# Placing the small Fourier sets of a fused filter and mixer next to each other on TensorE

## Chip, cores and metric

One NeuronCore of one Trainium2 chip runs the kernel. The metric is the device time in microseconds (us), from launch to end. The profile is one execution of the program, recorded by the hardware profiler. Everything is fp32.

## What is computed

The input x has 8 batches of 3008 tokens with 256 channels. First comes a global filter along the tokens (a real Fourier transform, a product with a learned complex filter, and the inverse transform), then one mixer layer:

```
X = np.fft.rfft(x, axis=1)
y = np.fft.irfft(X * (filt_r + 1j * filt_i), n=3008, axis=1)
h = relu(yT @ w_tok1) @ w_tok2          # across the tokens, 3008 -> 256 -> 3008
u = y + hT
out = u + relu(u @ w_ch1) @ w_ch2       # across the channels, 256 -> 1536 -> 256
```

## The kernel before

**The filter.** 3008 is 47 x 64. A set of length-64 sums runs first (`a_pair`), its result goes through DRAM, and then 16 pairs of frequency rows each get a forward length-47 set (`b_pair`), the product with the filter (the two VectorE instructions of line 674), a joining of the parts (`join`, lines 679 and 680) and an inverse length-47 set (`bi_pair`). The inverse set's two result banks are copied out by ScalarE (`by_block`, line 660), and SyncE's DMA queue writes them to DRAM (line 689). Each set is four small matmuls on the four quarters of the TensorE array (`four`, line 523); each takes both banks called `acc` and `b` in the order of `turn`. The length-64 sets have the same shape. The rest of the inverse transform is folded into the mixer's matmuls.

**The mixer.** The channel products use a seven-product scheme for 2x2 blocks (Strassen-Winograd), so a matrix product is seven matmuls with sums on VectorE before and after. The work is cut into 288 **items**: 8 batches, 6 token blocks m (the last of 448 columns, the others of 512), and 6 pairs of hidden tiles jp. Item i, in program order, does these things on TensorE: `up_first` (four matmuls, line 936) into two PSUM banks of the pool `pg`, which has exactly two buffers; `down` part 0 of the item before (three, line 970); `up_last` (three, line 952) into the same two `pg` banks; `down` part 1 of the item before (four, line 970). TensorE takes two passes for each fp32 matmul, and the profile has one record for a pass; an item thus has 28.

Beside it VectorE, whose sums all have line 914, does for each item: `up_middle` (two sums that read the `pg` banks, the first behind a ScalarE copy of line 939), `h_sums` (three sums that make the tile `t` for `down` part 1), and in `up_last` two sums that read the two `pg` banks into `hh`, each followed by a ReLU on ScalarE (line 957). The `pg` banks are free for the next item once these two are done.

**Once per block.** The next block's `u` tile is made in four **quarters** (`u_quarter`, lines 835 and 857, in banks `acc` and `b`), with sums on VectorE behind them, and then the steps `v_steps` (two, three sums). When a block ends, `finish` queues six **combining steps** `a`, `b_`, `c`, `d`, `turn(0)` and `store`; the last two are transposes (line 1002), and `store` issues the 16 output DMAs (line 1017). Queued steps are taken from the list `todo_v` by `one_step()`: one ahead of `h_sums`, one behind `up_last`, and two when a block's last `down` has been issued.

**The order.** Nothing reorders the program: it is written out by hand under `manual_schedule`. `mix` is a generator that yields after each third of an item (places 0, 1 and 2: after `down` part 0, after `up_last`, after `down` part 1), and the loop at the file's end uses those yields to advance another generator, `dft`, which makes the filter of the next group of batches. The groups are (0), (1, 2), (3, 4), (5, 6), (7). The filter of batches 1 and 2 runs in batch 0's items by a table of its own (its sets are of another form). The filters of (3, 4), (5, 6) and (7) run in batches 1 to 6. There `dft` says what is coming (`"a"` a length-64 set, `"w"` loads, `"b"` a forward set, `"m"` a joining, `"i"` an inverse set), and a table of (jp, place) says where it is due. Per block there are two pairs: forward sets at (5, 1) and (2, 1), joinings at (0, 1) and (3, 0), inverse sets at (1, 0) and (3, 2). In a batch's last block, "tail" below, one forward set comes at (1, 1). The quarters are at (3, 0), (4, 0) and (4, 2). In the tail of all batches but the last the token product of the next batch (line 802, 168 passes) runs at (2, 2), with its own sums on VectorE, and the quarters of the next batch's first block at (4, 0) and (5, 0).

The tiles that matter: `p1p` and `p2p`, the products' two halves, have one buffer each; the joining writes its result into the `p1p` tile, and the inverse set reads it from there. Tables (`wbp`) and filter rows have three buffers, the length-47 inputs (`t2p`) and the outputs (`t3p`) two.

Of the kernel before, what the change touches and what calls it, by code (L numbers as in the profile page):

```python
# [127 lines left out]
def kernel(  # L128
# [428 lines left out]
    def dft(bs):  # L557
# [102 lines left out]
            nc.scalar.copy(out=out.rearrange("p b (e g i) -> p b g e i", e=DH, i=CW),  # L660
                           in_=ps.rearrange("p b (g e i) -> p b g e i", e=DH, i=CW))

        def two_banks():
            return [bank(tag).rearrange("p (b d) -> p b d", b=2)[:, 0:nb, :] for tag in turn]

        def b_pair(c):
            pss, wb, t2 = two_banks(), wbs[c], t2s[c]
            four(lambda h, i: pss[h][half_of(i)], lambda h, i: wb[half_of(h, KH), i], lambda h, i: t2[half_of(h, KH), i])  # L670
            where = (p1p, p2p)
            for h in range(2):
                prods[c, h] = where[h].tile([P, 2, nb, D], FP32, tag="p%d" % (h + 1), name="p%d" % (h + 1))
                nc.vector.tensor_tensor(out=prods[c, h], in0=pss[h].unsqueeze(1).to_broadcast([P, 2, nb, D]),
                                        in1=filts[c % FB][:, :, 0, :].unsqueeze(2).to_broadcast([P, 2, nb, D]), op=ALU.mult)
# [3 lines left out]
            nc.vector.tensor_tensor(out=p1[:, 0], in0=p1[:, 0], in1=p2[:, 1], op=ALU.subtract)  # L679
            nc.vector.tensor_tensor(out=p1[:, 1], in0=p1[:, 1], in1=p2[:, 0], op=ALU.add)  # L680

        def bi_pair(c):
            pss, wb, p = two_banks(), wbs[c], prods.pop((c, 0))
            four(lambda i, h: pss[i][half_of(h)], lambda i, h: wb[half_of(i), 2 + h], lambda i, h: p[half_of(i), h])
            t3 = t3p.tile([P, KC, nb, D], FP32, tag="t3", name="t3")
            for i in range(KC):
                by_block(t3[:, i], pss[i])
            for h in range(2):
                nc.sync.dma_start(g_d[place_of[bs[0]][0]][ts(c, KC), ts(h, KH)].rearrange("k r b d -> r k b d"),
                                    t3[half_of(h, KH)])  # L690
# [8 lines left out]
        yield "w"  # L699
        yield "b"  # L700
        if not first:
            for c in range(K2 // KC):
                b_pair(c)
                if c + 2 < K2 // KC:
                    t2_load(c + 2)
                    w_load(c + 2)
                yield "m"
                join(c)
                yield "i"
                bi_pair(c)  # L710
                if c + 1 < K2 // KC:
                    yield "b"
            return
        if first:
# [244 lines left out]
    def down(m, jp, part, hh, t, po):  # L959
        hw = width(m) // 2  # L960
        if not po:
            for i in range(4):
                po.append(bank("po%d" % i).rearrange("p (s n) -> p s n", s=2))
        b11, b21, b22 = (hh[:, i, 0:hw] for i in (0, 3, 2))
        t1, t3, t2, t4_ = (t[:, i, 0:hw] for i in range(4))

        todo = (((0, 0, 1, 0, 1, b21), (0, 1, 0, 1, 2, b22), (2, 0, 1, 0, 0, b11)),
                ((1, 1, 1, 0, 6, t1), (3, 0, 1, 1, 4, t3), (2, 1, 0, 1, 5, t2), (1, 0, 0, 1, 3, t4_)))
        for i, j, first, last, n, mov in todo[part]:
            nc.tensor.matmul(po[i][:, j, 0:hw], chan[1][:, jp, n, :], mov, start=(jp == 0 and first == 1),  # L970
                             stop=(jp == JP - 1 and last == 1))
# [70 lines left out]
    def one_step():  # L1042
        if todo_v:
            todo_v.pop(0)()

    def mix(next_ready):

        wait = []
        pos, hhs, tts = {}, {}, {}

        def loads(b):
            if b + 1 < B and next_ready(b):
                for c in wait:
                    t4_load(b + 1, c)
                wait.clear()


        own = ({(4, 2): (0, 1)}, {(3, 0): (0,), (4, 0): (1,), (4, 2): (2, 3)})
        new = {(JP - 2, 0): (0, 1), (JP - 1, 0): (2, 3)}

        def u_parts(b, m, jp, place):
            parts = own[b > 0] if m + 1 < MT else new if b + 1 < B else {}
            now = parts.get((jp, place), ())
            b, m = (b, m + 1) if m + 1 < MT else (b + 1, 0)
            for part in now:
                u_part(b, m, part)
            if now and now[-1] == max(p for ps in parts.values() for p in ps):
                if m:
                    wait.append(m)
                todo_v.extend(v_steps(b, m))  # L1070
                if b and (b, m) < (B - 1, MT - 2):
                    w2m_load((m + 2) % MT)

        to_dram = [f for m in range(MT) for f in w2_sums(m)]
        w1_todo, w1_out = w1_sums()
        items = [(b, m, jp) for b in range(B) for m in range(MT) for jp in range(JP)]
        n = MT * JP
        for i in range(len(items) + 1):
            now, old = i < len(items), i >= 1
            if JP - 2 <= i < JP + 2:  # L1080
                for _ in range(6 if i > JP - 2 else 1):
                    if w1_todo:
                        w1_todo.pop(0)()
            elif i >= 2 * JP and i % 2 and w1_out:
                w1_out.pop(0)()
            if i and ended[0] < len(tiles):
                convert_middle()
                convert_end(False)
                convert_middle()
            if now:  # L1090
                b, m, jp = items[i]
                if i % n == 0:
                    wait.append(0)
                w = width(m)
                hhs[i] = hp.tile([P, 4, 256], FP32, tag="hh", name="hh")
                g = [bank("pg").rearrange("p (s n) -> p s n", s=2) for _ in range(2)]
                s = up_first(jp, uts[b, m], vts[b, m], w, g)
                up_middle(hhs[i], w, g, s)
            while todo_h1:
                todo_h1.pop()()  # L1100
            one_step()
            if old:
                bo, mo, jo = items[i - 1]
                tts[i - 1] = tp.tile([P, 4, 256], FP32, tag="t", name="t")
                for f in h_sums(hhs[i - 1], tts[i - 1], width(mo)):
                    f()
                down(mo, jo, 0, hhs[i - 1], tts[i - 1], pos.setdefault((bo, mo), []))
            if now:
                u_parts(b, m, jp, 0)
            copies()  # L1110
            yield b, i % n, 0
            if ended[0] < len(tiles):
                if i == 0:
                    convert_middle()
                convert_end(False)
            if now:
                up_last(jp, uts[b, m], vts[b, m], w, g, s, hhs[i])
                if b + 1 < B and i % n == n - 4:
                    t4_sums(b + 1, 0)
            one_step()  # L1120
            if now and i % n == n - 1:
                one_step()
            if now and b + 1 < B:
                if n - 4 - W1S <= i % n < n - 4:
                    w1_load(i % n - (n - 4 - W1S))
                if i % n == n - 4:
                    t4_sums(b + 1, 1)
            copies()
            loads(b)
            yield b, i % n, 1  # L1130
            if old:
                down(mo, jo, 1, hhs.pop(i - 1), tts.pop(i - 1), pos[bo, mo])
                if jo == JP - 1:
                    todo_v.extend(finish(bo, mo, uts[bo, mo], pos[bo, mo]))
                    one_step()
                    one_step()
            if now:
                if b + 1 < B and i % n == n - 4:
                    h1s[b + 1] = token_product(b + 1)
                u_parts(b, m, jp, 2)  # L1140
                if jp == JP - 1:
                    while todo_v and m + 1 == MT:
                        one_step()
                if i >= 8 and to_dram:
                    to_dram.pop(0)()
                if i in (28, 29):
                    w2m_load(i - 28)
            loads(b)
            yield b, i % n, 2
        while todo_v:  # L1150
            one_step()

    with tc.manual_schedule():
# [70 lines left out]
        for b, i, place in mix(next_ready):  # L1224
# [8 lines left out]
                continue  # L1233
            jp = i % JP
            if coming in "aw":
                due = place == 1 or group == 0
            elif group:
                due = (jp, place) in {"b": ((5, 1), (1 if i >= n - JP else 2, 1)), "m": ((0, 1), (3, 0)), "i": ((1, 0), (3, 2))}[coming]
            else:
                due = (jp - (coming == "i")) % JP in ((5, 1, 2, 3) if i < 4 * JP else (5, 0, 1, 2, 3)) and place == {"b": 1, "m": 2, "i": 0}[coming]  # L1240
            if coming == "a" and group == 0 and i < JP - 1:
                due = (2, 0, 1)[place]
            for _ in range(due):
                if not done:
                    coming = next(todo, "end")
# [31 lines left out]
```

## Time and profile before

| | |
|---|---|
| Time, median of 3 runs | 2445.72 us (2444.69 to 2446.33) |
| Profiled execution: time, span | 2445.61 us, 2443.8 us |
| Granted TensorE clock, mean | 0.995 |
| TensorE matmul busy | 2399.8 us in 12340 passes |
| VectorE busy | 1937.0 us |
| ScalarE busy | 687.0 us |
| GpSimd busy | 621.0 us |
| Items of batches 1 to 7 | 476.8 to 2425.0 us of the span |

The span runs from the first instruction to the last; the launch adds 1.8 us outside it. The items of batch 0, with the filter of batches 1 and 2 and the conversion of weights between them, fill the span up to 476.8 us. An item's length is read in the timeline as the distance between two starts of `ps_pg<-u` on line 936, the first passes of `up_first`.

In a timeline line the first number is the start in us from the span's start, the second the length in us, then the engine (PE is TensorE, DVE VectorE, ACT ScalarE), the line, the operation, its output and inputs, sizes, and how many instructions were merged. A bracket gives idle time of the engine ahead of the line, and what ended it. In a list of waits each line is: engine, the line waiting, the work waited for, us in total, times, longest.

### The profile page before, as it was taken

The page shows a single profiled execution, that of the slowest core. Times are in us where ns is not written, and L with a number is a line of the kernel's source. Part 1 is how long each engine was busy: PE and PEld are TensorE (multiplying, and loading weights), DVE is VectorE, ACT ScalarE, POOL GpSimd, SP SyncE. Part 2 cuts the span into 40 slices and gives each one's busy share as a digit, 9 for nine tenths or more (in the row PEclk, how much of TensorE's full clock was granted, in tenths as well). Part 3 has the DMA queues.
Part 4 walks back from the last instruction along what each step waited for, and adds up shares of the span by engine and source line. Part 5 has one row for each costly group of instructions (what it writes and reads, how often), then busy time and mean ns, then how long its engine had stood idle before and what let it go on. Part 6 is the DMA issues. An engine that isn't in the chain of part 4 may idle for free.

```text
span 2443.8 us, 35574 instructions
## 1 busy us (share of the span) xinstructions
PE 2399.8 (98%) x12340; PEld 1971.9 (81%) x12340; DVE 1937.0 (79%) x3684; ACT 687.0 (28%) x1355; POOL 621.0 (25%) x1115
## 2 busy tenths in 40 slices
PE   7999999999999999999999999999999999999998
PEld 4666676978788877987888878897889888898887
DVE  7798788787887788778878887877787787777776
ACT  5733223132222222123222222213221222212222
POOL 7476332122112211211211122112112112112121
PEclk8999999999999999999999999999999999999999
DMA  9985446453352222445344322433324121411100
GB/s 215 249 231 170 147 148 180 157 160 108 113 150 90 74 86 79 158 128 158 97 118 122 87 81 73 156 96 118 101 78 149 50 72 47 148 62 31 38 15 20
DMA packets 187419, 278.65 MB, mean 114 GB/s; under 512 B 35485, under 2 KB 125291, under 8 KB 187240
## 3 DMA queue, kind: packets, MB, share of 16 engines
q1 hardware_dynamic: 140952, 212.56, 29.1%
q0 software_dynamic: 34688, 53.83, 8.2%
q10 hardware_dynamic: 11600, 10.00, 1.3%
q8 instruction: 98, 1.61, 0.3%
q14 instruction: 81, 0.66, 0.1%
HBM read 193.52 MB, written 82.72 MB: 113 GB/s over the span
## 4 chain that ended last, share of the span: by engine, by line
PE 88%; DVE 6%; DMA 3%; issue 1%; ACT 1%; POOL 0%; SPq 0%; ACTq 0%; DVEq 0%; POOLq 0%
PE ps_po L970 33%; PE ps_pg L936 18%; PE ps_pg L952 14%; PE ps_b L523 5%; PE ps_b L802 3%; PE ps_acc L857 3%; PE ps_acc L802 2%; PE ps_b L857 2%; PE ps_b L835 2%; PE ps_acc L835 2%; DVE t L914 1%; PE ps_acc L523 1%; PE ps_b L751 1%; DVE hh L914 1%; DMA st<-in_moe_w_tok_dram 1%
## 5 line engine op out<-in xcount | busy, mean ns | idle before, releaser
L1017 POOL DMA_DIRECT2D out_dram<-r x752 | 408.2, 550 | 1636.0 <-ACT hh L957 1157.1
L914 DVE TENSOR_TENSOR hh<-ps_pg,s 128x512 f32<-128x512 f32 (+3 forms) x864 | 481.6, 585 | 230.7 <-ACT s L939 227.9
L957 ACT ACTIVATE hh<-hh 128x512 f32<-128x512 f32 (+1 forms) x576 | 347.7, 621 | 951.0 <-DVE hh L914 947.1
L970 PE MATMUL ps_po<-t,wc 128*128 128x256 f32 (+1 forms) x2304 | 546.8, 380 | 5.0 <-DVE t L914 4.0
L970 PEld LDWEIGHTS ps_po<-t,wc 128*128 128x128 f32 x2304 | 426.4, 190 | 130.9 <-DVE t L914 45.1
L970 PE MATMUL ps_po<-hh,wc 128*128 128x256 f32 (+1 forms) x1728 | 414.0, 375 | 1.4 <-POOL wc L382 0.8
L936 PE MATMUL ps_pg<-v,wc 128*128 128x256 f32 (+1 forms) x1728 | 413.4, 375 | 0.2 <-DVE v L914 0.2
L970 PEld LDWEIGHTS ps_po<-hh,wc 128*128 128x128 f32 x1728 | 326.5, 190 | 42.9 <-ACT s L939 3.4
L936 PEld LDWEIGHTS ps_pg<-v,wc 128*128 128x128 f32 x1728 | 326.8, 190 | 40.9 <-DVE v L914 3.2
L952 PE MATMUL ps_pg<-u,wc 128*128 128x256 f32 (+1 forms) x1152 | 295.2, 379 | 0.6 <-DVE hh L914 0.4
L952 PEld LDWEIGHTS ps_pg<-u,wc 128*128 128x128 f32 x1152 | 214.9, 190 | 57.5 <-DVE hh L914 25.8
L914 DVE TENSOR_TENSOR t<-t,hh 128x256 f32<-128x256 f32 (+1 forms) x576 | 244.9, 425 | 19.8
L914 DVE TENSOR_TENSOR s<-ps_pg,hh 128x512 f32<-128x512 f32 (+1 forms) x288 | 196.0, 681 | 30.7 <-DVE hh L914 0.9
L939 ACT COPY s<-ps_pg 128x256 f32<-128x256 f32 (+1 forms) x288 | 105.9, 368 | 335.5 <-PE ps_pg L936 332.5
L914 DVE TENSOR_TENSOR t<-hh 128x512 f32<-128x512 f32 (+1 forms) x288 | 194.0, 674 | 0.6 <-ACT hh L957 0.6
L936 PE MATMUL ps_pg<-u,wc 128*128 128x256 f32 (+1 forms) x576 | 171.8, 380 | 3.4 <-DVE hh L914 3.4
L952 PE MATMUL ps_pg<-v,wc 128*128 128x256 f32 (+1 forms) x576 | 168.8, 375 | 0.0
L936 PEld LDWEIGHTS ps_pg<-u,wc 128*128 128x128 f32 x576 | 106.2, 190 | 35.1 <-DVE hh L914 20.1
L914 DVE TENSOR_TENSOR u<-ps_acc,u 128x256 f32<-128x256 f32 (+1 forms) x84 | 46.2, 549 | 94.0 <-PE ps_acc L857 86.6
L952 PEld LDWEIGHTS ps_pg<-v,wc 128*128 128x128 f32 x576 | 109.2, 190 | 12.6
L914 DVE TENSOR_TENSOR u<-ps_b,u 128x512 f32<-128x512 f32 (+2 forms) x126 | 74.4, 591 | 28.9 <-PE ps_b L857 26.7
L857 PE MATMUL ps_acc<-w 128*128 128x256 f32 (+1 forms) x336 | 85.2, 376 | 0.0
(149 smaller groups left out, 2718.0 us busy)
## 6 DMA issues: line engine op xcount, KB each, us to landing
w<-w_tmp SPq DMA_DIRECT2D x84, 448.0 KB
w<-w_tmp SPq DMA_DIRECT2D x35, 896.0 KB
out_dram<-r POOLq DMA_DIRECT2D x696, 32.0 KB, 3.3
t<-g_tmp SPq DMA_DIRECT2D x42, 512.0 KB
g_tmp<-t SPq DMA_DIRECT2D x96, 192.0 KB
t<-z_tmp SPq DMA_DIRECT2D x180, 96.0 KB
z_tmp<-t SPq DMA_DIRECT2D x60, 256.0 KB
filt<-in_x_dram SPq DMA_DIRECT2D x90, 128.0 KB
```

Source lines behind the costliest of these rows:

```text
L523: nc.tensor.matmul(outs(i, j), stat(i, j), mov(i, j), start=True, stop=True)
L751: nc.tensor.matmul(acc[:, t, :], w1[:, a, ts(t, P)], t4[b, a // TC4][:, a % TC4, :], start=(a == 0 and t == 0), stop=(a == A - 1 and t == ...
L802: nc.tensor.matmul(ps[:, at], w[:, n], mov, start=(j == 0 and i in (0, 2)), stop=(j == AP - 1 and i >= 5))
L835: nc.tensor.matmul(ps[:, ds(q * P, n)], t4[b, c][:, r, ts(dh, P)], wai[:, 0:n], start=(first and q == 0), stop=(not first and q == 3))
L857: nc.tensor.matmul(ps[:, ds(j * hw, hw)], h1[:, n, :], w2m[m % 2][:, at, 0:hw], start=(i < 2 and j == 0), stop=(j == len(todo) - 1))
L914: nc.vector.tensor_tensor(out=out, in0=in0, in1=in1, op=op)
L936: nc.tensor.matmul(ps[:, 0:hw], chan[0][:, jp, n, :], mov, start=True, stop=True)
L939: nc.scalar.copy(out=s[:, 0], in_=g[0][:, 0, 0:hw])
L952: nc.tensor.matmul(ps[:, 0:hw], chan[0][:, jp, n, :], mov, start=True, stop=True)
L957: nc.scalar.activation(out=hs, in_=hs, func=AF.Relu)
L970: nc.tensor.matmul(po[i][:, j, 0:hw], chan[1][:, jp, n, :], mov, start=(jp == 0 and first == 1), stop=(jp == JP - 1 and last == 1))
L1017: q.dma_start(bass.AP(tensor=ob.tensor, offset=ob.offset + row * D + g * cw, ap=[[N1 * D, 32], [D if h else -D, n], [1, cw]]), blocks[ts(g ...
```

## The change

For the groups behind the first two (`tiled`), the inverse set of pair c-1 is issued directly behind the forward set of pair c, and takes its banks from the `pg` pool in place of `acc` and `b`; the products of pair c come behind it. Only the last inverse set of a group stands alone. `down` part 1 is cut into two parts of two matmuls, with a new yield between them (place 1.5), and the sets are due there. Forward sets are at (1, 1.5) and (4, 1.5), in the tail at (1, 1.5) and (3, 1.5); joinings at (3, 1), in the tail (2, 2), and (5, 1). The quarters move to (2, 2), (3, 0) and (3, 2). From batch 1 on, the combining steps are no longer taken ahead of `h_sums`, but two at a time behind `up_last`. Both `"w"` steps come at places of one item. Batch 0 is as it was, apart from the cut in `down`.

```diff
-        def b_pair(c):
-            pss, wb, t2 = two_banks(), wbs[c], t2s[c]
+        def b_pair(c):
+            pss, wb, t2 = two_banks(turn), wbs[c], t2s[c]
             four(lambda h, i: pss[h][half_of(i)], lambda h, i: wb[half_of(h, KH), i], lambda h, i: t2[half_of(h, KH), i])
+            return pss
+
+        def products(c, pss):
             where = (p1p, p2p)
...
-        def bi_pair(c):
-            pss, wb, p = two_banks(), wbs[c], prods.pop((c, 0))
+        def bi_pair(c, tags):
+            pss, wb, p = two_banks(tags), wbs[c], prods.pop((c, 0))
...
-            for c in range(K2 // KC):
-                b_pair(c)
-                if c + 2 < K2 // KC:
+            last = K2 // KC
+            for c in range(last):
+                pss = b_pair(c)
+                if c and tiled:
+                    bi_pair(c - 1, ("pg", "pg"))
+                products(c, pss)
+                if c + 2 < last:
                     t2_load(c + 2)
                     w_load(c + 2)
                 yield "m"
                 join(c)
-                yield "i"
-                bi_pair(c)
-                if c + 1 < K2 // KC:
+                if not tiled or c + 1 == last:
+                    yield "i"
+                    bi_pair(c, turn)
+                if c + 1 < last:
                     yield "b"
...
-                ((1, 1, 1, 0, 6, t1), (3, 0, 1, 1, 4, t3), (2, 1, 0, 1, 5, t2), (1, 0, 0, 1, 3, t4_)))
+                ((1, 1, 1, 0, 6, t1), (3, 0, 1, 1, 4, t3)), ((2, 1, 0, 1, 5, t2), (1, 0, 0, 1, 3, t4_)))
...
-        own = ({(4, 2): (0, 1)}, {(3, 0): (0,), (4, 0): (1,), (4, 2): (2, 3)})
+        own = ({(4, 2): (0, 1)}, {(2, 2): (0,), (3, 0): (1,), (3, 2): (2, 3)})
...
-            one_step()
+            if i < n:
+                one_step()
...
             one_step()
-            if now and i % n == n - 1:
+            if i >= n or i % n == n - 1:
                 one_step()
...
-                down(mo, jo, 1, hhs.pop(i - 1), tts.pop(i - 1), pos[bo, mo])
+                down(mo, jo, 1, hhs[i - 1], tts[i - 1], pos[bo, mo])
+            yield b, i % n, 1.5
+            if old:
+                down(mo, jo, 2, hhs.pop(i - 1), tts.pop(i - 1), pos[bo, mo])
...
-                due = place == 1 or group == 0
+                due = place == 1 or (place != 1.5 if group == 0 else coming == "w")
             elif group:
-                due = (jp, place) in {"b": ((5, 1), (1 if i >= n - JP else 2, 1)), "m": ((0, 1), (3, 0)), "i": ((1, 0), (3, 2))}[coming]
+                tail = i >= n - JP
+                due = (jp, place) in {"b": ((1, 1.5), (3 if tail else 4, 1.5)), "m": ((2, 2) if tail else (3, 1), (5, 1)),
+                                      "i": ((0, 1.5), (3 if tail else 4, 1.5))}[coming]
```

More of the change, by code (lines that the diff above doesn't have):

```diff
@@ L661, in by_block, with two_banks @@
                            in_=ps.rearrange("p b (g e i) -> p b g e i", e=DH, i=CW))
-        def two_banks():
-            return [bank(tag).rearrange("p (b d) -> p b d", b=2)[:, 0:nb, :] for tag in turn]
+        def two_banks(tags):
+            return [bank(tag).rearrange("p (b d) -> p b d", b=2)[:, 0:nb, :] for tag in tags]
         def b_pair(c):
-            pss, wb, t2 = two_banks(), wbs[c], t2s[c]
+            pss, wb, t2 = two_banks(turn), wbs[c], t2s[c]
             four(lambda h, i: pss[h][half_of(i)], lambda h, i: wb[half_of(h, KH), i], lambda h, i: t2[half_of(h, KH), i])
+            return pss
+        def products(c, pss):
             where = (p1p, p2p)
@@ L1241 @@
             if coming == "a" and group == 0 and i < JP - 1:
-                due = (2, 0, 1)[place]
+                due = {0: 2, 1: 0, 1.5: 0, 2: 1}[place]
             for _ in range(due):
```

## The prediction, on record before the changed kernel ran

> **What bounds the kernel.** I read the page first: busy time, then the chain that ended last.
>
> ```profile
> PE 2399.8 (98%) x12340; PEld 1971.9 (81%) x12340; DVE 1937.0 (79%) x3684; ACT 687.0 (28%) x1355; POOL 621.0 (25%) x1115
> ...
> PE 88%; DVE 6%; DMA 3%; issue 1%; ACT 1%; POOL 0%; SPq 0%; ACTq 0%; DVEq 0%; POOLq 0%
> ```
>
> TensorE is the bound, with VectorE next. But a busy TensorE need not be at its pace, so I went to the timeline. First an item of batch 2 with a forward set in it (TensorE lines alone):
>
> ```profile
> 829.94 0.59 PE L936 MATMUL ps_pg<-u,wc 128*128 128x256 f32 x2
> ...
> 834.35 0.65 PE L523 MATMUL ps_b<-t,wb 48*64 48x512 f32 x2
> ...
> 834.83 0.60 PE L523 MATMUL ps_b<-t,wb 48*64 48x512 f32 x2
> ...
> 835.37 1.99 PE L970 MATMUL ps_po<-t,wc 128*128 128x256 f32 x8
> ...
> 837.20 0.59 PE L936 MATMUL ps_pg<-u,wc 128*128 128x256 f32 x2
> ```
>
> The item lasts 837.20 - 829.94 = 7.26 us. An item without extras has 28 passes that start 0.216 apart, 6.04 us, and the trace has many of exactly that. **A set costs 1.22.** Its eight passes start in two groups of four, 0.48 apart, so the passes themselves are worth 0.96; the other 0.26 is at the edges (0.09 late into the set, the rest in the 0.52 after the second group and in a slow first pass behind it). In batches 5 and 6, where one batch is filtered and sets have 256 columns, items last 6.83, a set 0.79, its groups 0.27 apart: again 0.26 at the edges. Every set but seven costs this, wherever it stands.
>
> Second, a block without any filter work, batch 7, the second item after a block's end:
>
> ```profile
> 2237.28 0.68 DVE L914 TENSOR_TENSOR u<-ps_po,u 128x512 f32<-128x512 f32 x1
> ...
> 2237.95 0.59 PE L936 MATMUL ps_pg<-u,wc 128*128 128x256 f32 x2
> ...
> 2239.92 0.41 DVE L914 TENSOR_TENSOR hh<-ps_pg,s 128x256 f32<-128x256 f32 x1
> 2240.44 0.69 DVE L914 TENSOR_TENSOR s<-ps_pg,hh 128x512 f32<-128x512 f32 x1
> ...
> 2241.05 0.75 DVE L914 TENSOR_TENSOR u<-u,r 128x256 f32<-128x256 f32 x2
> ...
> 2241.72 0.68 DVE L914 TENSOR_TENSOR t<-hh 128x512 f32<-128x512 f32 x1
> ...
> 2242.55 1.97 PE L970 MATMUL ps_po<-t,wc 128*128 128x256 f32 x8
> 2243.23 1.28 DVE L914 TENSOR_TENSOR hh<-ps_pg,s 128x512 f32<-128x512 f32 x2
> ...
> 2244.35 0.59 PE L936 MATMUL ps_pg<-u,wc 128*128 128x256 f32 x2
> ```
>
> This item lasts 6.40: combining step `c` (the 0.75) stands ahead of the first sum for `t`, so `down` part 1 starts 0.35 late. The list of waits has it as
>
> ```profile
> PEld ps_po L970 <- DVE t L914: 45.1, 67, 0.8
> ```
>
> where 45.1 is mostly weight loads that merely come less early. The starts of all items of batches 1 to 7 show the real loss.
>
> **What the Trainium skill says.** The Trainium skill, "TensorEngine Tiling (Array Packing)", Key Properties: changing the tiling mode, "not just tile", drains the array, while different tiles run at once. The trace agrees: 0.26 per excursion, and four passes starting within 0.02. The page does not price the drain, nor say whether 48-row and 64-row weights share a mode; Tiling Modes lists 64 rows as the next size above 32, so both should be 64x64. The Trainium skill, "TensorE: Matmul & The Clock Gate", Part 2 (What happens when you issue a matmul): matmuls stay in program order and only weight loads are pulled ahead. So a set that waits for its banks holds all behind it. The Trainium skill's tiling page again, PSUM Bottleneck: evacuation may become the limit after packing; here one copy of a bank takes 0.58 on ScalarE, which is the row I use.
>
> **Part 1, the merged sets.** Three groups with 16 pairs each: 15 inverse sets per group directly follow a forward set, 45 in all, and one forward and one inverse stay alone. A follower that costs only its two groups saves 0.26. Bounds: nothing (a drain between the two kinds of set as between set and full matmul) to 0.36 (passes at the full pace of 0.43 for 512 columns, 1.22 - 0.86). I take 0.26, since passes one and two of one set already follow each other so, with other weights: **45 x 0.257 = 11.6 us**.
>
> **Part 2, do the sets wait?** From an item's start T: `up_first` 8 passes and `down` 0 with 6, so `up_last` starts at 3.02, `down` 1 at 4.32, its first half ends at 5.18, the forward set starts at 5.27, the inverse at 6.23, and the second half at 7.25; with its four passes (0.97, the first slow) the next item is at 8.22. The inverse set needs both `pg` banks, that is the end of VectorE's two `hh` sums. In the item shown they start 5.28 after T; without the 0.67 that `c` takes there, at 4.61, and end at 5.89. **Slack 0.3** at the worse of the two places (jp 1, behind `finish`); in an ordinary item they end at 5.5. Then ScalarE must copy both banks before `up_first` writes them. The wait of the copies shows in:
>
> ```profile
> 826.64 1.13 PE L952 MATMUL ps_pg<-u,wc 128*128 128x256 f32 x4
> ...
> 826.74 0.58 ACT L660 COPY t<-ps_b 128x512 f32<-128x512 f32 x1 [2.76 <-PE ps_acc L523]
> 827.22 0.59 ACT L660 COPY t<-ps_acc 128x512 f32<-128x512 f32 x1
> ```
>
> The first starts 0.10 after the full matmul behind a set, the second 0.48 later: 7.35 to 7.93 and 7.83 to 8.42. The next item's first bank is wanted at 8.22, its second at 9.08: covered by 0.3 and 0.7, by the half of `down` between. Without that cover the price is 0.7 to 1.2 per merged set. So I take zero.
>
> The changed order adds a wait on VectorE: the first product writes the single `p1p` tile, which the inverse set reads, so it starts at 7.35 rather than about 6.4. Steps `c` and `d` run in that gap. Behind it queue the next item's `up_middle`; two products of 1.21 end at 9.76, where `up_middle` (at T + 1.53 in an ordinary item) wants 9.75. An item bears about 1.0 of lateness (its first `t` sum ends at 3.31, wanted at 4.32). Cost zero, and 0 to 0.3 per set if everything runs late.
>
> **Part 3, combining steps behind `up_last`.** The item shown gets its `t` at 3.77 instead of 4.45, and its stall goes. Losses of this kind, item by item over 6.04 plus extras: batch 7, 4 x 0.43 + 0.33 + 0.70 = 2.75; the last blocks of batches 2, 4 and 6, 0.70 each; other second items of batches 2, 4, 6: 0.78, 1.03, 0.43; first blocks of batches 1, 3, 5: 0.33 each; further 0.79 and 0.78 in batches 1 and 3. Sum 9.65. The `v_steps`, now together at jp 4, take the 0.08 at a block's start with them (in the 0.43). The 0.25 at the start of odd batches stays. Bounds 5 to 10; I take **9.6 gone**.
>
> **Part 4, what comes.** In the tails of batches 1, 3 and 5 the joining (two sums of 0.71) now stands behind the token product's last sums and ahead of the next item's `up_middle`. In batch 1's trace those end 1.55 after that item's start, so `up_middle` comes 1.4 late, beyond the 1.0 borne, and `up_last`, `down` and the inverse set each wait some: about 1.2 where 0.47 is lost now, 0.75 twice and 0.5 in batch 5. The first block after each tail inherits a joining at (5, 1): 0.25, three times. The 448-column blocks with sets in their second item have no slack: 0.1 to 0.2 thrice. **3.0 added**; bounds 0 to 6.
>
> **Moved and free.** Splitting `down` adds no instruction. Quarters an item earlier: same passes, their sums have room (item jp 3 lasts 10 us), their table load is issued earlier. In SyncE's queue the two output DMAs of an inverse set now precede the loads for pair c + 2, which go out some 1.2 later and have two pairs, over 40 us. On GpSimd the clearing of filter rows comes ahead of a `store`. A group's last inverse set ends one item, about 10 us, later, and with it the loads of the next batch's token input; in batch 2 these start at 988 and are first wanted at 1014, with data moving until 1004: covered, and a miss would cost at most some us twice. VectorE's sum per block is about 42 us against TensorE's 45.4: under the bound, but not by much.
>
> **Sum.** 2445.6 (span 2443.8 and 1.8 around it, the median is 2445.7) - 11.6 - 9.6 + 3.0 = **2427.5**, -0.75%.
>
> **Rivals.**
> (1) *The sets drain between each other anyhow*, or VectorE's stalls reappear elsewhere: only one of the two gains comes. Without the first 2439, without the second 2434; for the first speaks that no two sets touch in this trace, against it the equal quarters.
> (2) *Evacuation*: if a set's copies are released together, or queue behind a late ReLU, `up_first` waits 0.3 per merged set, 13.5: 2441. Against it: ScalarE is busy 28%.
> (3) *Slower: the inverse set waits for VectorE's `hh` sums.* In today's second items of batch 2 the first `up_middle` sum comes 3.03 after the start, 1.5 late, behind a joining and `finish`. If VectorE is that late at both places, the `hh` sums end near 6.9, the set waits 0.7, and everything behind it does: 45 x 0.7 = 31.5, 2459. It decides from 0.4 per set (18 us / 45); 0.5 makes it slower by 0.2%. For it: VectorE at some 92% in these blocks. Against it: the joinings moved to items without `finish`.
>
> **Chances.** Both gains (2421 to 2433): 0.57. One of them, or one with partial waits (2433 to 2441): 0.22. Nothing left (within 0.2%, about what a measurement of this kernel can tell from no change, 2441 to 2450): 0.08. Rival 3: 0.13. The range starts at 2421 (part 1 at its upper bound, 4.6 more) and reaches to 2443.
>
> **What would show it.** Items with a merged set in batch 2 should last 8.22, groups of passes 0.48 apart all through; blocks with filter work 45.4 instead of 46.1, batch 7's second items 6.04 instead of 6.40. Line 523 or 936 waiting for line 914 or 660 by more than 0.2 each time would prove me wrong, as would an item with a set above 8.5, or passes over 0.6 apart where forward meets inverse.

## The result, and the profile after

The changed kernel takes 2425.94 us (median of 4 runs, 2425.36 to 2426.3) where the kernel before takes 2446.02 beside it (its three runs above and a fourth): ratio 0.9918, 95% interval 0.9901 to 0.9935. The forecast was 2427.5. The profiled execution took 2425.85 with a span of 2424.1; the one of before had 2443.8, so 19.7 us went. Batch 0 ends at 476.8 in both. All of the gain lies in batches 1 to 7.

In the changed file the lines behind the filter's functions are 8 higher: `up_first` is line 944, `up_last` 960, `down` 978, the sums 922; the products are line 677, 3 higher. The page:

```profile
PE 2382.0 (98%) x12340; PEld 1985.9 (82%) x12340; DVE 1942.6 (80%) x3684; ACT 686.5 (28%) x1355; POOL 619.6 (26%) x1115
...
PE 90%; DVE 4%; DMA 2%; ACT 1%; issue 1%; POOL 1%; SPq 0%; ACTq 0%; DVEq 0%; POOLq 0%
```

The same 12340 passes and 3684 VectorE instructions are there, VectorE's share of the chain fell from 6% to 4%, and TensorE still shows 98%: its share could not tell how much there was to gain. The list of waits has the one shown before at a quarter:

```profile
PEld ps_po L978 <- DVE t L922: 10.9, 17, 0.8
```

The timeline of batch 2's second item of block 1, with a merged set, weight loads left out:

```profile
819.51 0.59 PE L944 MATMUL ps_pg<-u,wc 128*128 128x256 f32 x2
...
823.83 1.03 PE L978 MATMUL ps_po<-t,wc 128*128 128x256 f32 x4
824.13 1.28 DVE L922 TENSOR_TENSOR hh<-ps_pg,s 128x512 f32<-128x512 f32 x2
...
824.78 0.65 PE L523 MATMUL ps_b<-t,wb 48*64 48x512 f32 x2
...
825.26 0.60 PE L523 MATMUL ps_b<-t,wb 48*64 48x512 f32 x2
...
825.69 1.04 PE L523 MATMUL ps_pg<-p,wb 64*64 64x512 f32 x8
...
826.66 1.13 PE L978 MATMUL ps_po<-t,wc 128*128 128x256 f32 x4
826.77 1.07 ACT L660 COPY t<-ps_pg 128x512 f32<-128x512 f32 x2 [0.70 <-PE ps_pg L523]
826.83 1.23 DVE L677 TENSOR_TENSOR p<-ps_b,filt 128x1024 f32<-128x1024 f32 x1 [0.15 <-PE ps_pg L523]
...
827.63 0.59 PE L944 MATMUL ps_pg<-u,wc 128*128 128x256 f32 x2
```

Against the forecast's timetable: the forward set starts 5.27 after the item (said: 5.27), the `hh` sums end at 5.90 (5.89), the copies start 0.11 after the full matmul behind the sets (0.10), and the product waits for the inverse set. But the inverse set starts 0.43 behind the forward set's second group, not 0.48, and the item lasts 8.12 instead of 8.22. The two sets together cost 8.12 - 6.04 = 2.08 where two single ones of 1.217 cost 2.43: before rounding, a merger saves 0.36, not 0.26.

Batch 7, the second item of block 1:

```profile
2220.50 0.59 PE L944 MATMUL ps_pg<-u,wc 128*128 128x256 f32 x2
...
2223.59 0.68 DVE L922 TENSOR_TENSOR t<-hh 128x512 f32<-128x512 f32 x1
...
2224.82 1.89 PE L978 MATMUL ps_po<-t,wc 128*128 128x256 f32 x8
...
2226.31 1.35 DVE L922 TENSOR_TENSOR u<-u,r 128x256 f32<-128x256 f32 x3
2226.54 0.59 PE L944 MATMUL ps_pg<-u,wc 128*128 128x256 f32 x2
```

The first sum for `t` starts 3.09 after the item, not 3.77, `down` part 1 at 4.32 without a wait, and the steps `c` and `d` (the 1.35) come behind. The item lasts 6.04.

Where the 19.7 went, from the starts of all passes in the two traces: 12.7 in the merged sets (45 mergers would give 16.0; 3.3 of that is lost in waits), 9.5 in the first two items of the blocks (10.3 of stalls went, but the first items of batches 2, 4 and 6 now last 5.92 instead of 5.67, as those of the odd batches do), and 2.4 given back elsewhere.

### The profile page after: what moved, and what is told of

The parts are those of the page before. It is cut to its first block, busy times and chain, and to the rows that moved or that the text cites. A ratio compares the mean times of both kernels' runs of the same rounds, so it can differ in the third digit from the quotient of the medians.

```text
span 2424.1 us, 35550 instructions
## 1 busy us (share of the span) xinstructions
PE 2382.0 (98%) x12340; PEld 1985.9 (82%) x12340; DVE 1942.6 (80%) x3684; ACT 686.5 (28%) x1355; POOL 619.6 (26%) x1115
## 4 chain that ended last, share of the span: by engine, by line
PE 90%; DVE 4%; DMA 2%; ACT 1%; issue 1%; POOL 1%; SPq 0%; ACTq 0%; DVEq 0%; POOLq 0%
PE ps_po L978 33%; PE ps_pg L944 18%; PE ps_pg L960 14%; PE ps_b L523 4%; PE ps_b L810 3%; PE ps_acc L865 3%; PE ps_acc L810 2%; PE ps_b L865 2%; PE ps_b L843 2%; PE ps_acc L843 2%; PE ps_pg L523 1%; PE ps_b L759 1%; DVE t L922 1%; DVE hh L922 1%; DMA filt<-in_x_dram 1%
## 5 line engine op out<-in xcount | busy, mean ns | idle before, releaser
L978 PE MATMUL ps_po<-t,wc 128*128 128x256 f32 (+1 forms) x2304 | 553.5, 379 | 1.8 <-DVE t L922 1.8
L960 PEld LDWEIGHTS ps_pg<-v,wc 128*128 128x128 f32 x576 | 109.1, 190 | 12.7
```

The source lines that it names most:

```text
L960: nc.tensor.matmul(ps[:, 0:hw], chan[0][:, jp, n, :], mov, start=True, stop=True)
```

## The experiments

Each is an edit to one of the two kernels. Times are medians beside the kernel before on the same chip (2445.84 for the first four, 2445.09 for the next four, 2445.62 for the last two). Where a run is set against the changed kernel, that is the 2425.94 of the result, unless a time of the changed kernel beside it is given.

**The steps alone.** In the kernel before:

```diff
-            one_step()
+            if i < n:
+                one_step()
...
-            if now and i % n == n - 1:
+            if i >= n or i % n == n - 1:
                 one_step()
```

> The kernel before, with nothing changed but the combining steps: from batch 1 on none ahead of the t sums, two behind up_last. Theory (the steps and the merged sets are two separate gains): the stalls in the second items of blocks go, 9 us or so; 2437 (2435 to 2439), and batch 7's second items last 6.04 instead of 6.40. Rival (the steps only pay together with the moved quarters and joinings, because they now run into the next item's sums): 2442 to 2446.

Measured: 2440.82, ratio 0.9978 (0.997 to 0.9987). That is between the theory and the rival: 5 us, half of what I had put on it. The second items of batch 7 do last 6.04. But its first items went from 6.12 to 6.24:

```profile
2229.24 0.59 PE L936 MATMUL ps_pg<-u,wc 128*128 128x256 f32 x2
2229.29 0.89 DVE L914 TENSOR_TENSOR v<-v,u 128x256 f32<-128x256 f32 x2
2229.77 1.56 PE L936 MATMUL ps_pg<-v,wc 128*128 128x256 f32 x6
```

`up_first`'s second matmul needs the sums of `v_steps` (the 0.89), which start after the item does: with the quarters still at (4, 2), both `v_steps` now come behind `up_last` of a block's last item. In the changed kernel the quarters end one item earlier, and so do these steps. In batch 4's blocks with filter work the stall in the second item only shrank from 0.2 to 0.14: there VectorE is late for another reason too: in the trace the joining of (0, 1) stands ahead of the sums of `finish`, and the first `up_middle` sum comes only 3.15 after the item's start.

**The merger without the steps.** In the changed kernel, both edits above undone.

> The changed kernel with the combining steps put back, one ahead of the t sums and one behind up_last. Theory (separate gains): the changed kernel's 2426 and the 9 to 10 us of stalls again, 2435.5 (2433 to 2438). Rival (they need each other: with step c ahead the hh sums end at 6.5 instead of 5.9 after the item's start and the inverse set waits for its banks at each jp 1): 2440 or more.

Measured: 2449.39, ratio 1.0016 (1.0009 to 1.0023): slower than the kernel before. The rival was right, by a wide margin. Batch 2, the same item as above:

```profile
822.86 0.59 PE L944 MATMUL ps_pg<-u,wc 128*128 128x256 f32 x2
...
825.96 0.75 DVE L922 TENSOR_TENSOR u<-u,r 128x256 f32<-128x256 f32 x2
826.63 0.69 DVE L922 TENSOR_TENSOR t<-hh 128x512 f32<-128x512 f32 x1
...
827.46 1.10 PE L978 MATMUL ps_po<-t,wc 128*128 128x256 f32 x4
828.15 1.28 DVE L922 TENSOR_TENSOR hh<-ps_pg,s 128x512 f32<-128x512 f32 x2
...
829.40 1.16 PE L523 MATMUL ps_pg<-p,wb 64*64 64x512 f32 x8
...
831.46 0.59 PE L944 MATMUL ps_pg<-u,wc 128*128 128x256 f32 x2
```

Step `c` (the 0.75) delays `t`, `down` starts 4.60 after the item instead of 4.32, its first passes are slow as well, and the item lasts 8.60 instead of 8.12: 0.36 in `down`, which second items without a set lose in this kernel too (6.40 instead of 6.04 in batch 7), and 0.12 in the set, whose second `pg` bank comes free at 829.43. In the kernel before, an inverse set stood at (1, 0), ahead of `up_last`; its 1.22 us gave VectorE time for `t`, and so a stall of 0.2 was all that showed. Moving the sets into `down` takes that cover away. The one-batch blocks of batch 6 show it best: in the kernel before, the second item with an inverse set has no stall at all (6.83, a set over 6.04), and here it loses 0.67 against the changed kernel (8.17 instead of 7.50). So the gain of the steps depends on where the sets are: worth 5 before, 23 behind the merger.

**Forward and inverse set apart.** In the changed kernel, a yield between the two; the forward set is due at place 1:

```diff
                 if c and tiled:
+                    yield "x"
                     bi_pair(c - 1, ("pg", "pg"))
...
-                due = (jp, place) in {"b": ((1, 1.5), (3 if tail else 4, 1.5)), "m": ((2, 2) if tail else (3, 1), (5, 1)),
+                due = (jp, place) in {"b": ((1, 1), (3 if tail else 4, 1)), "x": ((1, 1.5), (3 if tail else 4, 1.5)), "m": ((2, 2) if tail else (3, 1), (5, 1)),
```

> The changed kernel with the forward set moved ahead of the first half of down part 1, so that four full passes lie between it and the inverse set; the banks, the steps and all else stay. Theory (what the merger saves is one trip into and out of the small tiles, 0.36 each as the passes of the changed kernel show): 45 x 0.36 = 16 us come back, less 2 or so, since the inverse set now starts later and waits less for its banks; 2439.5 (2438 to 2443). Rival (the gain comes from where the sets stand, in the middle of down, not from their touching): 2426 to 2430.

Measured: 2439.12, ratio 0.9971 (0.9961 to 0.998). As the theory said. In batch 2:

```profile
827.45 0.60 PE L523 MATMUL ps_b<-t,wb 48*64 48x512 f32 x2
827.46 0.60 PE L523 MATMUL ps_acc<-t,wb 48*64 48x512 f32 x2
827.99 1.13 PE L979 MATMUL ps_po<-t,wc 128*128 128x256 f32 x4
829.05 1.09 PE L523 MATMUL ps_pg<-p,wb 64*64 64x512 f32 x8
830.07 1.13 PE L979 MATMUL ps_po<-t,wc 128*128 128x256 f32 x4
```

Four full passes stand between the sets, and each set pays its own way in and out: items of 8.48. Nothing else in the order of work changed. That the sets touch is worth 8.48 - 8.12 = 0.36 per pair, and 13 us in the whole kernel.

**The inverse set first.**

```diff
-                pss = b_pair(c)
                 if c and tiled:
                     bi_pair(c - 1, ("pg", "pg"))
+                pss = b_pair(c)
```

> The changed kernel with the two sets of a merged pair in the other order, the inverse one first. Theory (the inverse set can start when the hh sums have read the two pg banks, 5.9 after the item's start at jp 1 and 5.5 at jp 4, and the forward set's two groups are what covers that): it starts at 5.27 at the earliest, so it waits 0.7 at jp 1 and 0.3 at jp 4, some 22 x 0.7 + 23 x 0.3 less the 0.2 that one-batch sets wait already: 21 us more, 2446 (2440 to 2449). Rival (the banks are free in time in either order, and a set's waits come from elsewhere): 2425 to 2428.

Measured: 2446.90, ratio 1.0005 (0.9997 to 1.0014): no gain is left over the kernel before, and it is 21 us over the changed kernel, as the theory said. This is the forecast's slower rival in a pure form: a set that meets VectorE's `hh` sums too early costs all that the change brings. In batch 2:

```profile
829.45 1.28 DVE L922 TENSOR_TENSOR hh<-ps_pg,s 128x512 f32<-128x512 f32 x2
...
830.19 1.24 PE L523 MATMUL ps_pg<-p,wb 64*64 64x512 f32 x6
...
831.10 0.60 PE L523 MATMUL ps_b<-t,wb 48*64 48x512 f32 x2
831.27 0.60 PE L523 MATMUL ps_pg<-p,wb 64*64 64x512 f32 x2
```

The set starts once the first `hh` sum is done, and its part in the second bank follows only when the second sum is, at 830.73.

**No cover for the copies.** Both halves of `down` part 1 ahead of the sets:

```diff
                 down(mo, jo, 1, hhs[i - 1], tts[i - 1], pos[bo, mo])
+                down(mo, jo, 2, hhs[i - 1], tts[i - 1], pos[bo, mo])
             yield b, i % n, 1.5
```

> The changed kernel with the merged sets behind the whole of down part 1 instead of in its middle, so that the next item's up_first comes directly behind the inverse set. Theory (the half of down behind the sets is what hides ScalarE's copies out of the pg banks): up_first waits until the first copy is out, 0.10 + 0.58 + 0.1 after the sets, of which 0.1 hides the slow first pass: 0.68 for 30 pairs of two batches, 0.45 for 15 of one batch (copies of 0.35), less the 0.2 that seven inverse sets of one batch now wait; 25 us more, 2451 (2446 to 2455). Rival (the copies cost nothing, the place in the middle of down is of no account): 2425 to 2428.

Measured: 2453.20, ratio 1.0029 (1.002 to 1.0038); the profiled execution took 2450.69. In batch 2:

```profile
830.13 1.04 PE L523 MATMUL ps_pg<-p,wb 64*64 64x512 f32 x8
831.21 1.07 ACT L660 COPY t<-ps_pg 128x512 f32<-128x512 f32 x2 [1.56 <-PE ps_pg L523]
...
831.84 0.70 PE L944 MATMUL ps_pg<-u,wc 128*128 128x256 f32 x2 [0.67 <-ACT t L660]
```

Each item with a merged set of two batches lasts 8.76 (8.12 in the changed kernel) and the next one 0.1 more. So two matmuls of `down` hide what would be worth more than the whole change.

**What is left in the changed kernel.** Three of its waits were tried. First the inverse sets of the one-batch group, which lose 0.23 in second items (7.50 instead of 7.27); `down` is cut once more, and for that group all sets come behind its third matmul:

```diff
+            yield b, i % n, 1.75
+            if old:
+                down(mo, jo, 3, hhs.pop(i - 1), tts.pop(i - 1), pos[bo, mo])
...
+                at = 1.75 if group == 3 else 1.5
```

> The changed kernel with the sets of the one-batch group behind three of the four matmuls of down part 1 instead of two. Theory (at jp 1 these inverse sets come at 5.80 after the item's start, as their forward sets have 256 columns, while the hh sums end at 5.9): the wait of 0.23 in batch 6's second items goes, 7.50 becomes 7.27 (the one matmul left, 0.54, just covers a copy of 0.35 and 0.1 to 0.2 around it); 1.5 to 2 us less in all, 2424. Rival (the 0.23 is a cost of the shorter passes themselves): 7.50 stays.

Measured: 2425.08, one run. The 7.50 did become 7.27: the wait was for the `hh` sums. But the item behind each such set grew by 0.1, as one matmul doesn't quite cover the copies. The items of batches 5 and 6 sum to 1.1 us less; one run's time can't show that.

Second, the joining in the tails:

```diff
+                to_join.append(lambda: join(c))
                 yield "m"
-                join(c)
+                now_join()
...
                 t4_sums(b, j + 2)
+            if j == 6:
+                middle()
```

> The changed kernel with the joining of a tail's (2, 2) issued inside the token product, behind its seventh step, where VectorE idles between sums, instead of behind it. Theory (the joining makes the next item's up_middle 1.4 late): the items (5, 3) of batches 1 and 3 fall from 8.54 to 7.4 us, batch 5's from 7.58 to 6.5, the token product stays within 0.3; 3 us less, 2423. Rival (the sums of finish_h1 and the token product's own are what is late there): 8.2 or more stays.

`now_join` issues what stands in the list `to_join`, if it isn't out yet. Measured: 2423.37, one run. The items (5, 3) of batches 1 and 3 fell from 8.54 to 7.38 us, batch 5's from 7.58 to 6.91, and the token products stayed within 0.02. The theory holds for these items, though one run can't show what the whole time gained; batch 5 gave less than I said, since its inverse set still waits for an `hh` sum.

Third, the length-64 sets merged as well:

```diff
+    def a_two(u, u2, sd, sd2):
+        both = [[bank(tag) for tag in tags] for tags in (turn, ("pg", "pg"))]
+        for pss, s in zip(both, (sd, sd2)):
+            four(lambda h, e: pss[h][half_of(e)], lambda h, e: was[half_of(h), e], lambda h, e: s[half_of(h), e])
+        z = t2p.tile([P, 2, XC, D], FP32, tag="t2", name="z")
+        for (b, c), pss in ((u2, both[1]), (u, both[0])):
+            for h in range(2):
+                z_out(b, pss[h], 2 * c + h, nc.sync, z[:, h] if pss is both[1] else None)
...
+            if coming == "A":
+                due = jp % 2 and place == 1.5
```

> The changed kernel with the length-64 sets merged too: two of them directly behind each other in every second item, amid down, the second in the pg banks, whose copies are taken first (15 merged pairs in place of 30 single sets). Theory (0.36 for each trip into the small tiles that is saved, whatever the set): 15 x 0.36 = 5.4, and the 0.6 in the third item of batches 1, 3 and 5, where a quarter waits for a bank of a length-64 set; 6 us less, 2420 (2418 to 2423). Rival (four copies of some 0.5 each on ScalarE per pair are late for the next user of the banks): 2424 to 2430.

Measured: 2424.92, ratio 0.9912 (0.9895 to 0.9928): not told apart from the changed kernel, on the rival's side. Each merged pair saves its 0.36, and the 0.6 in the third items of batches 1, 3 and 5 is gone, but five items with quarters behind the sets last 13.41. ScalarE copies the `pg` banks first, and there a quarter needs `acc`:

```profile
505.29 1.13 PE L993 MATMUL ps_po<-t,wc 128*128 128x256 f32 x4
505.39 1.07 ACT L540 COPY z<-ps_pg 128x512 f32<-128x512 f32 x2 [0.79 <-PE ps_pg L523]
506.35 0.60 ACT L540 COPY t<-ps_b 128x512 f32<-128x512 f32 x1
506.83 0.62 ACT L540 COPY t<-ps_acc 128x512 f32<-128x512 f32 x1
507.50 1.16 PE L858 MATMUL ps_acc<-wai,t 128*128 128x128 f32 x8 [1.08 <-ACT t L540]
```

**Both together, with the copies in order of need.** The tail's joining and the merged length-64 sets, and at jp 3:

```diff
-        for (b, c), pss in ((u2, both[1]), (u, both[0])):
+        for (b, c), pss in ((u2, both[1]), (u, both[0]))[::-1 if jp == 3 else 1]:
```

> The changed kernel with both: the tail's joining inside the token product, and the length-64 sets merged two by two; where two quarters follow them (jp 3) ScalarE now copies the banks acc and b first. Theory (a trip into the small tiles is 0.36; every wait left is for a bank, so the copies' order decides): the 1.34 at five third quarters becomes 0 to 0.3, 15 x 0.36 for the length-64 sets and 3 for the tails come in full; 2415.5 (2414 to 2418), and the items (0, 3) and (1, 3) of batch 1 last 12.1 to 12.4 instead of 13.41. Rival (ScalarE has no room for four copies, whatever their order): 2421 or more.

> The changed kernel itself, on the same chip as the version with both, so that those two can be compared: 2426 (2425 to 2427).

Measured: 2415.43, ratio to the kernel before 0.9876 (0.986 to 0.9891); the changed kernel beside it 2427.17, ratio 0.9923 (0.991 to 0.9935), just above the range I gave. The item of 13.41 is now 12.06:

```profile
505.35 0.59 ACT L548 COPY t<-ps_b 128x512 f32<-128x512 f32 x1
...
505.83 0.59 ACT L548 COPY t<-ps_acc 128x512 f32<-128x512 f32 x1
506.10 1.13 PE L1004 MATMUL ps_po<-t,wc 128*128 128x256 f32 x4
506.31 1.09 ACT L548 COPY z<-ps_pg 128x512 f32<-128x512 f32 x2
507.07 1.05 PE L869 MATMUL ps_acc<-wai,t 128*128 128x128 f32 x8
```

The copies of `b` and `acc` are out when the quarter comes at 507.07, and those of `pg` are needed only three us later, at the next item's start. As the theory said, the order of the copies decides, and this version beats both kernels.

## Why the prediction was right, step by step

**What bounds it, right.** TensorE was and is the bound, and the loss was in the edges of the sets and in late sums, not in idle time that the page shows.

**Part 1, right mechanism, mis-sized term.** I took the 0.26 that lies outside the two groups' 0.48 each, and gave 0.36 as the upper bound. The upper bound came: between the two sets the passes run on at 0.43, the full pace for 512 columns, and it is the step from a set's first group to its second that is slow by 0.05 when it comes out of full matmuls. Apart and together differ by 0.36 on the chip. In sum 12.7 instead of 11.6, closer than the term deserves: 45 mergers at 0.36 are 16.0, and 3.3 us of waits, most of which I had put at zero, took back most of the difference. The Trainium skill, "TensorEngine Tiling (Array Packing)", Key Properties, says that a change of mode drains the array and a change of tile does not. The runs agree: the step from 48-row to 64-row weights took 0.43, as long as the next step within the inverse set, and each trip out of the full array cost 0.36.

**Part 2, right for two batches, wrong for one.** For 512 columns the slack of 0.3 was 0.28, and no wait came in the plain blocks. For the one-batch group I reused that timetable, but a forward set of 256 columns is over in 0.48 us instead of 0.91, so its inverse set is at the banks before the `hh` sums, which end at 1958.06 in this item of batch 6:

```profile
1956.78 1.28 DVE L922 TENSOR_TENSOR hh<-ps_pg,s 128x512 f32<-128x512 f32 x2
...
1957.92 0.85 PE L523 MATMUL ps_pg<-p,wb 64*64 64x256 f32 x8
```

The set starts at 1957.92 and stretches to 0.85 us. Such waits, 0.23 in most plain blocks and more in the tail, are most of the 3.3 us; by the forecast's own sign (line 523 waiting for the sums by more than 0.2 each time), this part was wrong for that group. The cover for the copies held, and the run without it shows its price.

**Part 3, right in sum, wrong as an account of causes.** 9.6 was forecast and 9.5 came, in the changed kernel as a whole, and the nearness is in part luck. 10.3 of stalls went, since the list left out the second items of the first blocks of batches 2 and 4 (7.62 in the kernel before, 0.36 over an item with a set); the three 0.25 that took some of it back are those forecast in part 4. And I had taken the steps' gain as a thing apart, and priced a kernel with only the mergers at 2434; the 3.0 of part 4 was left out of that sum, which with it is 2437. It is 2449. The step that failed is the list of stalls, which I read off the kernel before: there the inverse set ahead of `up_last` covered part of VectorE's lateness, and the change takes that cover away. The steps by themselves give 5, since the `v_steps` need the quarters' move and the joinings of the kernel before make VectorE late too. The other half of rival 1 was right to the microsecond: 2439 was said for a kernel without the mergers' gain, and the run with the sets apart took 2439.12.

**Part 4, right in size by chance.** 3.0 was forecast (its terms add up to 3.05 to 3.35). 2.4 came, or 3.1 with the three 0.25, which came as forecast. But the terms were others. The items behind the tails' token products in batches 1 and 3 do lose 1.2 as worked out (8.54 instead of 7.38), confirmed by moving the joining; yet the token products lose less than before (24.42 and 24.29 instead of 24.83), and the tails' net share of the 2.4 is only 0.6. The other 1.8 is three times 0.6 that I had not seen, in the third item of batches 1, 3 and 5: a quarter, now soon behind a length-64 set, waits for ScalarE's second copy out of that set's banks. In batch 1:

```profile
495.88 0.59 ACT L539 COPY t<-ps_acc 128x512 f32<-128x512 f32 x1
...
496.52 1.13 PE L865 MATMUL ps_acc<-w 128*128 128x256 f32 x4 [0.33 <-ACT t L539]
```

I had called the move of the quarters free. So the total is nearer to the forecast, 1.6 us, than its parts are.

**Rivals 2 and 3.** Rival 2 did not come, and rival 3 came only on a small scale, in the waits of part 2. But both are real mechanisms: the copies without cover cost 27 us, and the inverse set ahead of VectorE's sums 21. In the forecast's timetable the margin to either is 0.3 us.

Not tried: whether the 0.05 of a set's first group belongs to the weights' load; the profile doesn't say.

## What to carry to other kernels

Put small matmuls that share one shape of tile next to each other: here each trip into the quarters and back cost 0.36 us, with 256 columns as with 512, and a busy share of 98% hid it. Then price the place: ask which work in front gives the next engine its time, and which work behind covers the copies, because a set that is moved takes its cover along. A stall list from the kernel before prices only the kernel before; when two parts of a change touch the same cover, try each without the other before giving either its own number.

## What the runs showed of the hardware that I had not expected

In the run with the inverse set first, the passes of the forward set's first two matmuls start at 831.10, ahead of the inverse set's last at 831.27, although they come later in the program: by these starts the two halves of the array's rows, each of which writes one of the two banks, went on at their own times, each in order, and only the half whose bank was late waited. By the Trainium skill, "TensorE: Matmul & The Clock Gate", Part 3 (The mechanism), matmuls start and end in program order; the recorded starts here do not, by 0.17 us. So the forecast's "holds all behind it" was too strong: here only the late half was held. The full-array matmul behind them did come after both: it starts at 832.66, 0.52 after the late half's last passes and 1.12 after the other half's.
